# A fused gated-memory and mixture-of-experts kernel: list writes spread one by one, routing steps and weight splits at other places in the attention loop

## Chip, cores and metric

The kernel runs on one NeuronCore of one Trainium2 chip. The metric is the device time of one execution in microseconds (us), the median of the runs; less is better.

## What is computed

First a recurrent memory with exponential gates, over 4 batches, 8 heads, 768 steps and 40 columns per head. Then its 3072 output rows of 320 columns go through a two-level mixture of experts: a group (of 4) and an expert in the group (of 4) are picked by argmax, and each row is multiplied through that one expert, 320 to 1024 to 320, all in float32.

```python
for t in range(S):
    m_new = np.maximum(f_gate[:, :, t] + m, i_gate[:, :, t])
    C = f_stab * C + i_stab * np.einsum('bhd,bhe->bhde', vt, kt)
    n = f_stab * n + i_stab * kt
    y[:, :, t] = sigmoid(o_gate[:, :, t]) * (C @ qt) / np.maximum(np.abs(n @ qt), 1.0)
x = y.transpose(0, 2, 1, 3).reshape(B * S, H * D)
...
g_idx = np.argmax(x @ w_group, axis=1)
e_idx = np.argmax(xg @ w_expert[g], axis=1)
h = np.maximum(xg[mask_e] @ w1[g, e], 0.0)
out[tok_idx] = (g_w * e_w)[:, None] * (h @ w2[g, e])
```

## The kernel before

**Attention in 24 units.** A unit is one chunk of 128 steps of one batch, `u = 4 * chunk + batch`, units 0 to 23. `unit(u)` (line 795) is software-pipelined by hand, and each engine runs in the order in which the code is written. A unit loads the inputs of unit u+3 (tiles `qk`, `nt`), makes the scores of u on TensorE (`sp`), turns the finished rows of u-2 (`av<-x`, line 264), masks the scores on VectorE (`pt`, two halves, line 187), transposes the values of u-1 back (`av<-avs`), divides them on VectorE (`den`, then `xn`) and, up to unit 18, multiplies them on GpSimd into the rows `x` (line 258; from unit 19 on VectorE does that). GpSimd also scales the value rows of u+1 (`vscale`, tile `vz`, line 171), which need `nt` of that unit.

**Routing in the gaps.** After every fourth unit `logits_of` multiplies the rows by the gate matrix, and `route` (line 311) turns the logits of a set of units into a list entry per token. The sets are units 0-3, 4-7, 8-11, 12-15, 16-17, 18-21 and 22-23. `route` is a generator: each `yield` is a step of one or two small VectorE instructions (`mx`, `df`, `eq`, `oh`, rank matmul, `pr`, `slf`, `slot`, `sm`, `sg`, `se`, `ent`, `ohs`, `ohsum`). `chores` is a list of such generators, and `go_on(n)` (line 398) runs n steps of the first. The tables `FIRST`, `RANKS` and `MID` (lines 849 to 851) say how many steps each unit runs, and where in it. `first_experts` (line 457) picks the two fullest experts after the first two sets; it ends in `ewi`, the numbers that SyncE needs to load those experts' weights.

**List puts.** `put_id` (line 444) takes one unit's 128 entries and scatters them into the table `itab` in DRAM: an indirect DMA whose descriptors GpSimd writes, after a one-element memset of `sep`. Before the change every unit up to 15 puts at most one, units 16 and 17 at most two, and from unit 18 on a unit puts all that are there. When the puts of units 0 to 17 are through, SyncE reads the first expert's list back (`load_ix(0)`, tile `ix`), and GpSimd gathers its first 256 rows (`load_x`, tile `xg`). TensorE turns these rows and starts expert (0,0), while units 22 and 23 are still being routed.

**Weight splits.** Weights are split into a high and a low part in the type fp32r: `split_tasks` (line 600) lets ScalarE cast the high part (`w1h`, `wsk`, `w2h`) and puts the subtraction for the low part (`w1l`, `wsk`, `w2l`, VectorE, line 609) into the list `lows`, which `do(lows)` empties. `SPLITS` (line 852) says which units cast a part.

**After the units.** `expert((0, 0), ...)` (line 1015) runs between its matmuls four functions: `last_turn`, `last_logits`, `last_ranks` (line 981) and `last_slots` (line 996), and in the middle of its last block of the second product `late_half` (line 1007). Tokens of units 18 to 23 that belong to the first expert come in through `late_x`: VectorE makes a selection matrix per unit (`late`, line 377, a step at the end of `route`), and TensorE multiplies the rows by it (line 771). The result, split into `xhl` (lines 776, 777), is the input of expert (0,1), which has the same weights and 112 slots. Its hidden products (lines 693 to 697) go through `hs` (ACT line 698, DVE line 699) before the relu. Then experts (1,0) to (15,0) follow, each some 10 to 17 us of TensorE.

Of the kernel before, what the change touches and what calls it, by code (L numbers as in the profile page):

```python
# [61 lines left out]
def lstm_moe(ctx: ExitStack, tc: tile.TileContext, gates, qkT, nat, wcat, w1, w2, cst, seq, out):  # L62
# [59 lines left out]
    rt = {"manual": True}  # L122
# [658 lines left out]
    def run(stage, u):  # L781
        if 0 <= u < NU:
            stage(u)
# [11 lines left out]
    def unit(u):  # L795
        run(loads, u + 3)
        if u == 6:
            first_tokens()
        run(scores, u)
        run(turn, u - 2)  # L800
        go_on(FIRST.get(u, 0))
        run(lambda v: masked(v, 0), u)
        run(lambda v: masked(v, 1), u)
        if u == 0:
            busy(5)
        run(carried, u)
        run(state, u)
        run(back, u - 1)
        run(norm, u - 1)
        run(rows, u - 1)  # L810
        if u < B:
            run(rows2, u - 1)
        if u < NU - 2:
            run(vscale, u + 1)
        if u == NU - 3:
            run(vscale, u + 2)
        if u >= B:
            run(rows2, u - 1)
        if u < 12:
            sum_on(SUMS.get(u, 1))  # L820
        do(lows)
        go_on(RANKS.get(u, 0))
        if u % B == 1 and 1 < u < EUNITS:
            logits_of(u - 5, u - 1)
        if u == EUNITS + 1:
            logits_of(EUNITS - 2, EUNITS)
        if u == NU - 1:
            logits_of(EUNITS, NU - 2)
        if u == 10:
            go_on(2)  # L830
            chores.insert(0, first_experts())
        if u == EUNITS + 3:
            chores.append(early_counts())
        go_on(MID.get(u, 0))
        gate_o(u)
        do(early_splits, SPLITS.get(u, 0))
        run(state2, u)
        run(values, u)
        do(backs)
        if u == 3:  # L840
            first_entries()
        if u == 5:
            first_rows()
        for _ in range(len(ids) if u >= EUNITS else min(rt.get("old", 0), 1 if u < 16 else 2)):
            put_id()
        rt["old"] = len(ids)

    SUMS = {1: 2, 4: 2}
    FIRST = {6: 4, 10: 4, 14: 4, 18: 4, 20: 4}
    RANKS = {6: 1, 10: 1, 14: 1, 18: 1, 20: 1}  # L850
    MID = {6: 2, 7: 3, 8: 4, 10: 3, 11: 5, 12: 6, 13: 7, 14: 2, 15: 3, 16: 2, 17: 2, 18: 5, 19: 4, 20: 8, 21: 4, 22: 1}
    SPLITS = {15: 1, 16: 1, 17: 1, 20: 1, 22: 1}

    def gate_sums(lo, hi):
        fg, ig = G[:, 0, lo:hi], G[:, 1, lo:hi]
# [88 lines left out]
    with tc.manual_schedule():  # L944
        for u in range(5, NU):
            if u == NU - 1:
                rt["turns"] = turn_tasks((0, 0), EARLY, xgs[0], Cp)
            unit(u)
            if u == EUNITS + 2:
                assert not ids and len(unordered["ids"]) == EUNITS  # L950
                load_ix(0)
            do(early_loads, {12: 2, 13: 2, 15: 1, 16: 1, 17: 1, 18: 1, 20: 1, 21: 2, 22: 1, 23: 4}.get(u, 0))
            if u == NU - 3:
                xgs[0] = load_x(EARLY, ix_of(0), True)
# [24 lines left out]
            do(early_splits, 1)  # L979

        def last_ranks():
            go_on(8)
            do(early_splits)
            while ids:
                put_id()
# [10 lines left out]
        def last_slots():  # L996
            rt["experts"] = all_experts()
            next(rt["experts"])
            load_e(2, [ET.SP, ET.Pool])
            load_w1(2)  # L1000
            load_ix(2)
            load_w2(2, nc.gpsimd)
            for v in range(EUNITS, NU - 2):
                add(v)
            do(split, 1)

        def late_half():
            add(NU - 2)
            add(NU - 1)
            halves()  # L1010
            do(lows)
            do(split, 2)
            do(lows)

        expert((0, 0), EARLY, wsp_[0], xgs[0], ix_of(0), [last_turn, last_logits, last_ranks, last_slots], last=[late_half])
# [253 lines left out]
```

## Time and profile before

| | us |
|---|---|
| median of 3 runs | 379.28 (378.10 to 381.99) |
| the profiled execution, whole | 383.42 |
| its span, first to last instruction | 381.8 |
| TensorE busy in the span | 358.4 |
| VectorE, ScalarE, GpSimd busy | 248.0, 188.6, 143.0 |
| mean granted TensorE clock | 0.976 of full speed |

All rows below come from the one profiled execution, in us from the span's start. PE is TensorE's matmul, PEld its weight load, DVE VectorE, ACT ScalarE, POOL GpSimd, SP SyncE; L448 is line 448 of the kernel. In a timeline row stand start, busy time, engine, line, operation, output<-input and, in brackets, how long the engine was idle before and what ended that. "issue" is idle time for which the profile shows no cause.

### The profile page before, as it was taken

The numbers are of one execution on the slowest core, as the hardware profiler recorded it, in microseconds if no ns is written. First come the engines' busy times: TensorE is split into PE (matmuls) and PEld (weight loads), VectorE is DVE, ScalarE is ACT, GpSimd is POOL, SyncE is SP. The second block draws the span as 40 slices with busy tenths as digits, with TensorE's granted clock in tenths as the row PEclk, the third lists the DMA queues.
The fourth block names the chain that finished last, engine by engine and source line by source line (L and its number), as shares of the span: only waits on it lengthen the run. The fifth ranks groups of instructions, "written<-read, shape, count | busy, mean of one in ns | idle before, by whom it ended". The sixth has DMA issues, their size and how long they took to land.

```text
span 381.8 us, 9441 instructions
## 1 busy us (share of the span) xinstructions
PE 358.4 (94%) x3572; PEld 322.2 (84%) x3572; DVE 248.0 (65%) x639; ACT 188.6 (49%) x459; POOL 143.0 (37%) x196
## 2 busy tenths in 40 slices
PE   7999999998879779799999999999999999999993
PEld 3777777776657679799999999999999999999992
DVE  5878978887757674748895847657556633554510
ACT  2444545464334441658755737467467542454520
POOL 1263445367754045552235081332413332234110
PEclk9999999999988999889999999999999999999997
DMA  7877678889566502957079975848623497668500
GB/s 201 291 262 231 179 234 255 269 284 284 189 195 195 215 21 49 340 192 262 33 253 403 370 259 174 277 169 308 232 81 131 161 339 272 229 230 323 186 20 16
DMA packets 27383, 82.23 MB, mean 215 GB/s; under 512 B 8800, under 2 KB 12339, under 8 KB 23746
## 3 DMA queue, kind: packets, MB, share of 16 engines
q1 hardware_dynamic: 18946, 63.21, 48.8%
q0 software_dynamic: 4560, 13.16, 10.1%
q10 hardware_dynamic: 3824, 5.18, 4.1%
q8 instruction: 30, 0.49, 0.5%
q14 instruction: 23, 0.19, 0.1%
HBM read 72.70 MB, written 9.10 MB: 214 GB/s over the span
## 4 chain that ended last, share of the span: by engine, by line
PE 68%; issue 10%; DVE 7%; DMA 6%; POOL 5%; ACT 1%; POOLq 1%; SPq 0%; DVEq 0%
PE psh L714 13%; PE psh L682 8%; PE po L737 7%; PE po L738 7%; PE po L736 7%; PE sp L182 3%; PE po L742 2%; PE avT L231 2%; PE av L239 2%; PE po L741 2%; POOL x L258 2%; PE av L264 2%; PE avT L222 2%; DMA xg<-x_d,ix 2%; DMA nt<-in_nat_dram 2%
## 5 line engine op out<-in xcount | busy, mean ns | idle before, releaser
L547 POOL DMA_INDIRECT out_dram<-y,ix x32 | 38.8, 1213 | 72.8 <-ACT y L748 58.0
L736 PE MATMUL po<-w2h,hh 128*128 128x320 f32 (+3 forms) x200 | 63.4, 317 | 0.0
L737 PE MATMUL po<-w2l,hh 128*128 128x320 f32 (+3 forms) x200 | 62.3, 311 | 0.0
L738 PE MATMUL po<-w2h,hh 128*128 128x320 f32 (+3 forms) x200 | 62.1, 311 | 0.0
L543 POOL DMA_INDIRECT xg<-x_d,ix x32 | 33.7, 1052 | 74.0 <-DMA ix<-itab 40.7
L609 DVE TENSOR_TENSOR w2l<-w2s,w2h 128x640 fp32r<-128x640 f32 x64 | 50.9, 825 | 13.2 <-ACT w2h L607 13.1
L671 DVE SCALAR_TENSOR_TENSOR hh<-psh,hh 128x240 fp32r<-128x240 f32 (+6 forms) x108 | 36.2, 366 | 20.0 <-ACT hh L668 18.1
L668 ACT ACTIVATE hh<-psh 128x288 fp32r<-128x288 f32 (+8 forms) x68 | 30.1, 444 | 31.7 <-PE psh L714 15.3
L607 ACT CAST w2h<-w2s 128x640 fp32r<-128x640 f32 x64 | 43.2, 721 | 0.0
L682 PE MATMUL psh<-xhl,w1s 128*128 128x144 f32 (+3 forms) x336 | 41.3, 283 | 0.0
L682 PEld LDWEIGHTS psh<-xhl,w1s 128*128 128x128 f32 x336 | 40.9, 191 | 0.0
L714 PE MATMUL psh<-xhl,w1h 128*128 128x256 f32 (+5 forms) x224 | 37.5, 288 | 0.4 <-DVE xhl L654 0.2
L748 ACT ACTIVATE y<-po,ix 128x320 f32<-128x320 f32 (+3 forms) x24 | 12.7, 529 | 50.0 <-PE po L738 43.2
L736 PEld LDWEIGHTS po<-w2h,hh 128*128 128x128 f32 (+3 forms) x200 | 36.5, 182 | 0.0
L737 PEld LDWEIGHTS po<-w2l,hh 128*128 128x128 f32 (+3 forms) x200 | 36.4, 182 | 0.0
L738 PEld LDWEIGHTS po<-w2h,hh 128*128 128x128 f32 (+3 forms) x200 | 36.3, 182 | 0.0
L187 DVE TENSOR_TENSOR pt<-sp,cs 128x512 f32<-128x512 f32 x48 | 30.7, 680 | 5.4 <-PE sp L182 4.2
L448 POOL DMA_INDIRECT itab<-ent,slot x24 | 25.0, 1044 | 23.2 <-DVE ohs L371 17.3
L714 PEld LDWEIGHTS psh<-xhl,w1h 128*128 128x128 f32 x224 | 31.2, 189 | 1.1 <-DVE xhl L654 0.4
L258 POOL TENSOR_TENSOR x<-xn,den 128x320 f32<-128x320 f32 x19 | 18.0, 946 | 37.6 <-DVE xn L253 32.6
L182 PE MATMUL sp<-qk 40*128 40x128 f32 x384 | 29.3, 290 | 0.4 <-issue 0.4
L231 PE MATMUL avT<-pt,vz 128*41 128x128 f32 x384 | 28.1, 283 | 1.4 <-issue 1.0
(215 smaller groups left out, 706.8 us busy)
## 6 DMA issues: line engine op xcount, KB each, us to landing
w1s<-in_w_dram SPq DMA_DIRECT2D x13, 1536.0 KB
w2s<-in_w_dram SPq DMA_DIRECT2D x13, 1280.0 KB
nt<-in_nat_dram SPq DMA_DIRECT2D x24, 480.0 KB
qk<-in_qkT_dram SPq DMA_DIRECT2D x48, 160.0 KB
x_d<-x ACTq DMA_DIRECT2D x24, 192.0 KB
w1s<-in_w_dram SPq DMA_DIRECT2D x8, 384.0 KB
w2s<-in_w_dram SPq DMA_DIRECT2D x8, 320.0 KB
w1s<-in_w_dram POOLq DMA_DIRECT2D x1, 1536.0 KB
```

Of the source, the lines that this page charges most:

```text
L182: mm(t["pm"][r][:, pr, :], qk[rs, 0, pr, :], qk[rs, 1, pr, :], start=True, stop=True)
L231: mm(placed(pr, r), t["vz"][:, head(pr, r), :], t["pm"][r][:, pr, :], start=(c == 0 and pr < 2), stop=True, skip_group_check=True)
L543: return nc.gpsimd.indirect_dma_start(out=o, out_offset=None, in_=src, in_offset=bass.IndirectOffsetOnAxis(ap=idx, axis=0))
L547: return nc.gpsimd.indirect_dma_start(out=out, out_offset=bass.IndirectOffsetOnAxis(ap=idx, axis=0), in_=y, in_offset=None, bounds_check=N ...
L607: nc.scalar.copy(a, src[:, s])
L609: lows.append(lambda: nc.vector.tensor_tensor(o[rows], src[rows, s], a[rows].bitcast(F32), op=ALU.subtract))
L671: nc.vector.scalar_tensor_tensor(hh[:, f:f + per, dst], src[:, :, t], 0.0, hr.bitcast(F32)[:, :, t], op0=ALU.max, op1=ALU.subtract)
L682: ins = mm(ps[:, g * W:(g + 1) * W], w1s[:, s], xhl[:, k, :], start=(k == 0), stop=(k == 2))
L714: ins = mm(ps[:, g * W:(g + 1) * W], w[:, s], x, start=(n == 0), stop=(n == len(todo) - 1))
L736: mm(po[0:m], hh[:, f, t], w2h[:, s], start=st0, stop=False)
L737: mm(po[0:m], hh[:, f, t], w2l[:, s], start=False, stop=False)
L738: ins = mm(po[0:m], hh[:, f, tl], w2h[:, s], start=False, stop=sp0)
```

## The change

Four edits, of which none adds or removes an instruction; they move some.

- Puts: each unit ends with one `put_id`, and from unit 16 on there is another between the value rows of the next unit (`vscale`) and the rows `x`. The loop that emptied the list is gone. `load_ix(0)` comes at the end of unit 21, not 20.
- Routing: `MID` gives other numbers, and `first_experts` waits behind the route of units 4-7 instead of going ahead of it, so that the sets 4-7, 8-11 and 12-15 have their entries sooner.
- Splits in the units: `do(lows)` stands behind the `MID` steps instead of ahead of the routing, and the three parts of the first expert's `w1` are cast in units 14, 15 and 16 instead of 15, 16 and 17.
- Behind the units: `last_ranks` finishes the second generator in `chores` (the route of units 18-21, of which its four `late` tiles are left) after one step of the first (units 22-23); `last_slots` splits two parts of the next expert's `w1` instead of one, with their lows, and `late_half` the third.

```diff
         if u == NU - 3:
             run(vscale, u + 2)
+        if u >= 16:
+            put_id()
         if u >= B:
             run(rows2, u - 1)
         if u < 12:
             sum_on(SUMS.get(u, 1))
-        do(lows)
         go_on(RANKS.get(u, 0))
...
             go_on(2)
-            chores.insert(0, first_experts())
+            chores.append(first_experts())
...
         go_on(MID.get(u, 0))
+        do(lows)
         gate_o(u)
         do(early_splits, SPLITS.get(u, 0))
...
-        for _ in range(len(ids) if u >= EUNITS else min(rt.get("old", 0), 1 if u < 16 else 2)):
-            put_id()
-        rt["old"] = len(ids)
+        put_id()
...
-    SPLITS = {15: 1, 16: 1, 17: 1, 20: 1, 22: 1}
+    SPLITS = {14: 1, 15: 1, 16: 1, 20: 1, 22: 1}
...
-            if u == EUNITS + 2:
+            if u == EUNITS + 3:
                 assert not ids and len(unordered["ids"]) == EUNITS
                 load_ix(0)
...
         def last_ranks():
-            go_on(8)
+            go_on(1)
+            while next(chores[1], StopIteration) is not StopIteration:
+                pass
+            chores.pop(1)
+            go_on(7)
...
-            do(split, 1)
+            do(split, 2)
+            do(lows)
 
         def late_half():
             add(NU - 2)
             add(NU - 1)
             halves()
-            do(lows)
-            do(split, 2)
+            do(split, 1)
             do(lows)
```

On GpSimd, from unit 19 to the gather of the first expert's rows. `ent_71` are the entries of units 12-15, `ent_72` those of units 16 and 17; `vz_104`, `vz_105` and `vz_106` are the value rows of units 21, 22 and 23. Before:

```order
L447 MEMSET sep 1x1
L448 DMA itab<-ent_71,slot 49168x4
L171 TENSOR_TENSOR vz_104<-nt,eb 128x8x40
L447 MEMSET sep 1x1
L448 DMA itab<-ent_72,slot 49168x4
L447 MEMSET sep 1x1
L448 DMA itab<-ent_72,slot 49168x4
L171 TENSOR_TENSOR vz_105<-nt,eb 128x8x40
L171 TENSOR_TENSOR vz_106<-nt,eb 128x8x40
L543 DMA xg<-x_d,ix 128x384 x2
```

After the change:

```order
L171 TENSOR_TENSOR vz_104<-nt,eb 128x8x40
L447 MEMSET sep 1x1
L448 DMA itab<-ent_71,slot 49168x4
L447 MEMSET sep 1x1
L448 DMA itab<-ent_72,slot 49168x4
L171 TENSOR_TENSOR vz_105<-nt,eb 128x8x40
L171 TENSOR_TENSOR vz_106<-nt,eb 128x8x40
L447 MEMSET sep 1x1
L448 DMA itab<-ent_72,slot 49168x4
L543 DMA xg<-x_d,ix 128x384 x2
```

The last of the 18 puts now stands behind the value rows of units 22 and 23. Before, four puts of `ent_71` stood in one row ahead of `vz_104`; now one is left there, the other three having gone out between earlier rows.

On VectorE, between two low parts `hh` of expert (0,0), in `last_ranks`. `late_2475` is the selection matrix of unit 18 before, `late_2453` to `late_2459` are those of units 18 to 21 in the change; `pr` to `sm` are steps of the route of units 22-23. Before:

```order
L671 SCALAR_TENSOR_TENSOR hh<-psh,hh 128x2x256
L355 TENSOR_TENSOR pr<-av,oh 128x32
L357 TENSOR_REDUCE slf<-pr 128x2
L360 CAST slot<-slf 128x2
L363 COPY cntf<-av 128x16
L384 TENSOR_REDUCE sm<-ex 128x10
L386 TENSOR_SCALAR sm<-sm 128x10
L387 RECIPROCAL sm<-sm 128x10
L391 TENSOR_TENSOR sg<-sm,oh_2417 128x8
L393 TENSOR_REDUCE se<-sg 128x2
L395 TENSOR_TENSOR ent_74<-sm,se 128x2
L377 TENSOR_SCALAR late_2475<-cs,late_f,slf 128x112
```

After the change:

```order
L671 SCALAR_TENSOR_TENSOR hh<-psh,hh 128x2x256
L377 TENSOR_SCALAR late_2453<-cs,late_f,slf 128x112
L377 TENSOR_SCALAR late_2455<-cs,late_f,slf 128x112
L377 TENSOR_SCALAR late_2457<-cs,late_f,slf 128x112
L377 TENSOR_SCALAR late_2459<-cs,late_f,slf 128x112
L355 TENSOR_TENSOR pr<-av,oh 128x32
L357 TENSOR_REDUCE slf<-pr 128x2
L360 CAST slot<-slf 128x2
L363 COPY cntf<-av 128x16
```

Four of the six `late` instructions moved ahead of the ten routing instructions.

On VectorE, from the choice of the next experts (`ewi`) to the first hidden product of expert (0,1) (`hs`). Before:

```order
L516 CAST ewi<-eidr 128x2
L777 TENSOR_TENSOR xhl<-av,xhl 128x3x112
L609 TENSOR_TENSOR w1l<-w1s,w1h 128x1024 x2
L609 TENSOR_TENSOR wsk<-w1s,wsk 64x1024
L699 TENSOR_TENSOR hs<-hs,psh 128x112 x2
```

After the change:

```order
L516 CAST ewi<-eidr 128x2
L609 TENSOR_TENSOR w1l<-w1s,w1h 128x1024 x2
L777 TENSOR_TENSOR xhl<-av,xhl 128x3x112
L609 TENSOR_TENSOR wsk<-w1s,wsk 64x1024
L699 TENSOR_TENSOR hs<-hs,psh 128x112 x2
```

Two subtractions of the next expert's `w1` moved ahead of the input of expert (0,1).

## Rows read from the trace of the kernel before

**Rows 1.** Windows: us, busy of PE, PEld, DVE, ACT, POOL, PEclk, DMA share, GB/s

```profile
104.40:111.20 6.80, 5.08 (x62) 3.21 (x60) 3.06 (x10) 2.33 (x7) 4.44 (x9) 0.99 0.83 248
111.20:118.00 6.80, 6.53 (x55) 5.05 (x55) 6.13 (x22) 2.28 (x8) 3.73 (x5) 0.51 0.11 38
...
159.00:165.80 6.80, 5.99 (x26) 5.79 (x26) 4.76 (x13) 3.98 (x12) 0.63 (x1) 0.51 0.50 187
...
169.00:375.00 206.00, 205.76 (x1537) 201.54 (x1536) 122.22 (x257) 113.66 (x233) 62.98 (x62) 1.00 0.62 224
```

**Rows 2.** The chain that ended last, 107 to 129 us: start, us, what

```profile
107.79 0.96 POOL itab L448
...
109.52 3.60 issue
...
113.36 1.00 POOL itab L448
...
114.67 2.78 DMA itab<-ent,slot
...
117.46 1.93 DMA ix<-itab
...
121.63 6.89 DMA xg<-x_d,ix
...
128.57 0.56 PE Cp L264 x3
```

**Rows 3.** Timeline of POOL: the rows x, the put that waits, the value rows

```profile
80.80 0.72 POOL L258 TENSOR_TENSOR x<-xn,den 128x320 f32<-128x320 f32 x1 [1.41 <-DVE xn L253]
...
84.98 1.64 POOL L258 TENSOR_TENSOR x<-xn,den 128x320 f32<-128x320 f32 x1 [0.98 <-DVE xn L253]
...
113.36 1.00 POOL L448 DMA_INDIRECT itab<-ent,slot  x1 [3.83 <-DVE ohs L371]
...
115.65 1.68 POOL L171 TENSOR_TENSOR vz<-nt,eb 128x320 f32<-128x320 f32 x2
```

**Rows 4.** Timeline of DVE, 82 to 113 us

```profile
84.82 1.22 DVE L609 TENSOR_TENSOR w1l<-w1s,w1h 128x1024 fp32r<-128x1024 f32 x1
...
109.83 0.17 DVE L246 TENSOR_TENSOR den<-av,floor 128x8 f32<-128x8 f32 x1 [3.57 <-PE avT L231]
...
112.92 0.16 DVE L395 TENSOR_TENSOR ent<-sm,se 128x2 f32<-128x2 f32 x1
```

**Rows 5.** Windows of one us at the end of the loads of the units

```profile
110.00:111.00 1.00, 0.73 (x13) 0.54 (x10) 0.90 (x4) 0.58 (x2) 0.00 (x0) 1.00 0.81 270
111.00:112.00 1.00, 0.53 (x3) 0.50 (x3) 0.93 (x6) 0.25 (x1) 0.00 (x0) 0.53 0.14 45
```

**Rows 6.** Timeline of DVE, 139 to 165 us

```profile
139.63 0.69 DVE L671 SCALAR_TENSOR_TENSOR hh<-psh,hh 128x512 fp32r<-128x512 f32 x1 [0.66 <-issue]
...
142.27 1.61 DVE L377 TENSOR_SCALAR late<-cs,late_f,slf 128x112 f32<-128x112 f32 x6
...
153.74 2.35 DVE L609 TENSOR_TENSOR w1l<-w1s,w1h 128x1024 fp32r<-128x1024 f32 x2
156.12 1.22 DVE L609 TENSOR_TENSOR wsk<-w1s,wsk 64x1024 fp32r<-64x1024 f32 x1
157.37 0.45 DVE L699 TENSOR_TENSOR hs<-hs,psh 128x112 f32<-128x112 f32 x2
...
159.64 0.45 DVE L699 TENSOR_TENSOR hs<-hs,psh 128x112 f32<-128x112 f32 x2
```

**Rows 7.** Waits of PE: engine line waited for: us in total, times, longest

```profile
PE psh L693 <- DVE hs L699: 2.3, 2, 1.5
PE av L771 <- DVE late L377: 2.0, 1, 2.0
PE av L264 <- POOL sep L447: 1.9, 2, 1.2
PE Cp L264 <- DMA xg<-x_d,ix: 1.4, 2, 1.2
```

More of the change, by code (lines that the diff above doesn't have):

```diff
@@ L850, in lstm_moe @@
     RANKS = {6: 1, 10: 1, 14: 1, 18: 1, 20: 1}
-    MID = {6: 2, 7: 3, 8: 4, 10: 3, 11: 5, 12: 6, 13: 7, 14: 2, 15: 3, 16: 2, 17: 2, 18: 5, 19: 4, 20: 8, 21: 4, 22: 1}
-    SPLITS = {15: 1, 16: 1, 17: 1, 20: 1, 22: 1}
+    MID = {6: 2, 7: 3, 8: 4, 10: 2, 11: 8, 12: 8, 13: 3, 14: 2, 15: 7, 18: 7, 19: 2, 20: 8, 21: 4, 22: 1}
+    SPLITS = {14: 1, 15: 1, 16: 1, 20: 1, 22: 1}
     def gate_sums(lo, hi):
```

## The prediction

> **What bounds the kernel now.** I read the windows by stage first, then the chain that ended last, then the timelines around its longest links. From 169 to 375 us TensorE is busy for 205.76 of 206.00 us at the full clock [rows 1]: no instruction there is touched, and whatever is late before 169 us is late at the end. So the change is worth what it saves between the first unit and 169 us. In that stretch the chain does not run along TensorE's matmuls but through the list of the first expert [rows 2]: put on GpSimd, landing of the put (2.78 us), SyncE's read of the list (1.93), the gather of the rows (6.89), and only then TensorE turns the rows, at 128.57. TensorE itself got there almost at the same time; it waited 1.4 us for these rows [rows 7]. Behind them it waits 2.0 us for `late` and 2.3 us for `hs` [rows 7], and twice it runs at half clock (1.2 instead of 2.4 GHz): from 111.2 to 118.0 us, behind a stretch in which it was busy for 5.08 of 6.80 us, and from 159.0 to 165.8 [rows 1].
>
> **A. The last put.** Before, the last two puts wait for `ent` of units 16-17, done at 113.08 [rows 4], and the second goes out at 114.67 [rows 2]. `ent` is that late because VectorE sat idle for 3.57 us until 109.83 [rows 4], while GpSimd worked off four puts in a row (one of them at 107.79, rows 2) and the DMA engines were at 0.83 of their time [rows 1]. The profile gives no cause: it puts the wait down to a matmul which itself came late, and calls the 3.60 us on the chain "issue" [rows 2]. I take it for a consequence of the row of puts. With three of these four puts gone out earlier, `ent` would be ready at about 113.08 - 3.6 = 109.5, the first put runs then, and the second would go at about 110.7. But in the new order it stands behind the value rows of units 22 and 23, and these need the inputs of unit 23. The loads end at about 111.3: the DMA share falls from 0.81 to 0.14 there [rows 5]. Of the two value rows (1.68 us together, rows 3) one can run sooner, so 111.3 + 0.84 + 0.25 for the `sep` memset puts the second put at 112.4. If SyncE's loads come 1.5 us sooner, because `x` and with it the stores in the same queue lanes come sooner, it is 110.9. So A is -2.3 to -3.8 us on this execution, and 0 if the stall comes back by another cause; I take -3.0. Landing, list read and gather follow at their old lengths. A quarter of one weight load now stands ahead of the list read in SyncE's queue; the DMA engines are nearly free by then (share 0.14, rows 5), which hides it.
>
> Two more edits lie in this stretch. `first_experts` behind the route makes `ewi` about five small instructions later (1.1 us by an estimate of 0.2 us each, from `ent` and `den` in rows 4), and SyncE's weight loads with it; that delays the loads of later units, and is the reason that I don't use the upper end of A. The other is VectorE's load. GpSimd's `x` takes 0.72 us alone and 1.64 beside a `w1l` of 1.22 [rows 3, 4], and TensorE waited 1.9 us in two units for such an `x` [rows 7]. In the new order three routing steps and more stand between `xn` and the low part in unit 15, but in units 16 and 17 no step is left to stand there, so two of the three still collide; unit 18 is free of it. Against that, unit 15 carries 8 routing instructions and the 1.22 us low part behind one another, some 3 us by the same estimate, in a unit of some 4 us in which the masks and divisions take 2. I count these as +1 and -2 us on TensorE, and 0 in the sum: TensorE will be early for the rows of the first expert anyhow, and the chain of puts hides both. If that cover is gone they are worth -1.
>
> **B. The clock.** With the stall gone TensorE would not fall to half clock at 111 us, and would reach the turn of the rows about 3.6 (stall) and 3.4 us (half of 6.8) sooner than the 127.2 of before (128.57 - 1.4): at about 120, while the rows land at 128.5 - 3.0 = 125.5. That is 5 us of idle time in one piece. Idle time of 6.80 - 5.08 = 1.7 us was followed by 6.8 us at half clock before [rows 1], so expert (0,0) will begin at half clock. A full such stretch costs half of its 6.8 us, 3.4. Part of it is hidden, since in expert (0,0) TensorE waits for VectorE's routing as well; I take +1.7, bounds 0 and +3.4.
>
> The Trainium skill (TensorE: Matmul & The Clock Gate, section HAM oscillation) warns of just this: a kernel whose matmul bursts are followed by a wait for a DMA has every burst begin cold. The rows at 111.2 us agree. By that rule B is the full +3.4, which is the third rival below.
>
> **C. The `late` matrices.** Six of them took 1.61 us at 142.27, behind ten routing instructions of units 22-23, and TensorE waited 2.0 us for them [rows 6, 7]. Now four stand straight behind the `hh` that ends at 140.32 (139.63 + 0.69). They take 4 x 0.27 = 1.1 us, so at 141.4 TensorE can begin. That is when its hidden products are done: its wait of 2.0 us ended with the fourth matrix, at 142.27 + 1.1 = 143.4, so it began at 141.4. The routing behind them is 1.1 us later, its put and the next experts' choice with it; expert (0,1) hides both, since TensorE's waits name neither [rows 7]. `w2l` and the last `hh` end when they did, because VectorE's work is the same in sum, and the second product needs them in its last quarters. C is -1.9; at worst 0, if they become the wait.
>
> **D. The input of expert (0,1).** Before, VectorE did two `w1l` (2.35 us) and `wsk` (1.22) between `xhl` and the first `hs` at 157.37 [rows 6]. Now the two run beside the second product of expert (0,0), where VectorE was idle, and 1.22 is left. ScalarE's cast of `wsk` comes first, so of 2.35 us about 1.9 are won beyond C. The four pairs of hidden products follow at 159.64 - 157.37 = 2.27 us each, bound by ScalarE and VectorE as before, so the head start reaches the end of the expert. D is -1.9. It is 0 if TensorE at half clock sets the end there again, and up to -3.6 if the stretch at 159.0 does not come back (half of 3.4).
>
> **The sum.** A -3.0, B +1.7, C -1.9, D -1.9 make -5.1, from 383.42 to 378.3 for the profiled execution. The timed runs before had a median of 379.28, 4.1 below the profiled one, which is about the length of the stall; I read this as a stall that is often shorter there, and take A as -2.2 for the median: -4.3, **375.0 us**.
>
> **Rivals.**
> 1. The chain isn't shortened: the stall comes from the load on the DMA engines and not from the row of puts, or the last put waits for the inputs of unit 23 as long as it waited for `ent`. Then A and B are about 0, and half of D goes at half clock: 379.28 - 1.9 - 1.0 = 376.4, and 378 with the `ewi` delay of 1.1. For it: the profile names no cause, and the loads end at 111.3 in either case. Against it: VectorE had nothing to do for 3.57 us.
> 2. The change does what it says and the half clock at 159 us does not return: D at -3.6, B at 0. 379.28 - 2.2 - 1.9 - 3.6 = 371.6. For it, the gap for `hs` that goes; against it, pairs of 2.27 us leave TensorE half idle, as before.
> 3. Slower: TensorE waits idle for the first expert's rows and is then at half clock for the whole of expert (0,0). The place is the turn of the rows. If the inputs of unit 23 land 4 us later than before, the last put goes at 112.4 + 4 = 116.4, later than now by 1.7; expert (0,0) costs 3.4 more, and expert (0,1), again half idle, 3.4 more than the one stretch that it has. 379.28 + 1.7 + 3.4 + 3.4 - 1.9 - 1.9 = 384.0. It decides from the point where the put is later than 114.7. Against it: with `x` sooner these loads should come sooner.
>
> **How the numbers follow.** I give the forecast 0.45, rival 1 0.30, rival 2 0.13 and rival 3 0.12. Within 1% (3.8 us, about what a measurement can tell from no change) lies 375.5 to 383.1. Of the forecast's 0.45 about 0.33 lies below 375.5, of rival 1 0.02, and all of rival 2: faster 0.48. Slower is rival 3 with its 0.12, and same the rest, 0.40. The range goes from 370.5, somewhat past rival 2, to 381.0, where rival 1 with a small delay is inside and rival 3 is left out.
>
> **What would show it.** Right: no row of three or more puts between 95 and 115 us; the second put of units 16-17 at 111 to 112.5 us; TensorE idle ahead of the turn of the rows for several us, and a half clock behind it; the wait of `av` for `late` gone; the first `hs` less than 3 us behind `xhl`. Wrong: an idle VectorE of more than 2 us near 106 to 110 us with single puts (A's cause), a put of units 16-17 at 114 us or later (rival 1 or 3), a wait of `po` for `w2l` or `hh` in expert (0,0) (C), or the stretch from `xhl` to the end of expert (0,1) as long as before (D).

## The result, and the profile after

The changed kernel took **382.06 us** (median of 20 runs, 380.27 to 385.57), the kernel before 380.06 beside it (20 runs): a ratio of 1.0055, 95% interval 1.0032 to 1.0077, where 375.0 was forecast. Its profiled execution took 381.87, with a span of 380.2 (383.42 and 381.8 before). So the profile after is its kernel's median, while the profile before is 3.4 us above its own: the two traces show a gain of 1.6 us and the medians a loss of 2.0. The 383.42 is none of the 20 timed executions, and the chip it ran on is not on record. Ratios here are over executions that nothing disturbed, so they can differ a little from the ratio of two medians; for g_after below only 5 of 12 are left by that rule, because one of them is very low (376.27), and over all 12 the medians, 382.05 and 381.06, give 1.0026.

Waits of PE in the changed kernel, 60 to 170 us (in us, times, longest):

```profile
PE Cp L264 <- DMA xg<-x_d,ix: 3.9, 1, 3.9
PE av L264 <- POOL sep L447: 2.0, 1, 2.0
PE psh L693 <- DVE hs L699: 1.9, 2, 1.1
...
PE av L771 <- DVE sm L384: 0.6, 1, 0.6
```

The wait for `late` [rows 7] is gone; that for the first expert's rows has gone from 1.4 to 3.9 us; and where two waits for `sep` (in truth for `x`, ahead of it on GpSimd) were 1.2 us at most, one of 2.0 stands now. (TensorE still begins on `late` 0.55 us behind its hidden products; the name `sm` is the profile's, and the four matrices had ended at 141.49, 0.75 us before it began.) GpSimd's timeline at the new wait and at the last put:

```profile
85.13 0.72 POOL L171 TENSOR_TENSOR vz<-nt,eb 128x320 f32<-128x320 f32 x1 [2.85 <-DMA nt<-in_nat_dram]
85.79 0.09 POOL L447 MEMSET sep<- 1x1 f32 x1
86.03 1.77 POOL L448 DMA_INDIRECT itab<-ent,slot  x1 [0.16 <-issue]
87.84 0.73 POOL L258 TENSOR_TENSOR x<-xn,den 128x320 f32<-128x320 f32 x1
...
112.18 0.97 POOL L448 DMA_INDIRECT itab<-ent,slot  x1 [2.71 <-DVE ohs L371]
113.18 0.72 POOL L171 TENSOR_TENSOR vz<-nt,eb 128x320 f32<-128x320 f32 x1
114.50 0.88 POOL L171 TENSOR_TENSOR vz<-nt,eb 128x320 f32<-128x320 f32 x1 [0.59 <-DMA nt<-in_nat_dram]
...
115.56 1.00 POOL L448 DMA_INDIRECT itab<-ent,slot  x1 [0.16 <-issue]
120.32 0.97 POOL L543 DMA_INDIRECT xg<-x_d,ix  x1 [3.76 <-DMA ix<-itab]
```

At unit 16 a value row waits 2.85 us for its input; the put that the change set behind it, and ahead of `x`, takes another 1.77; only then comes `x`, whose `xn` VectorE had finished at 85.67. The last put goes at 115.56, 0.9 later than before [rows 2], and the gather at 120.32 where it went at 120.33. The windows, with the granted clock as the third figure from the end:

```profile
88.60:95.40 6.80, 6.78 (x79) 4.90 (x79) 2.12 (x5) 2.03 (x7) 4.53 (x7) 0.50 0.93 280
126.20:133.00 6.80, 5.75 (x26) 5.39 (x27) 3.72 (x13) 1.84 (x5) 0.00 (x0) 0.50 0.36 142
160.30:163.70 3.40, 3.40 (x16) 3.36 (x15) 2.50 (x6) 1.80 (x5) 0.00 (x0) 0.50 0.66 252
169.00:375.00 206.00, 203.80 (x1520) 198.95 (x1518) 121.60 (x255) 112.98 (x232) 63.43 (x63) 1.00 0.61 219
```

The half clock at 111 us [rows 1] is gone, but TensorE is at half clock (1.2 GHz) from the end of the wait at unit 16, at 88.6, and from within the wait for the rows, at 126.2; the stretch at 159 is half as long. And the loads no longer end at 111 us [rows 5], but at about 115:

```profile
111.00:112.00 1.00, 1.00 (x21) 0.74 (x20) 0.86 (x6) 0.95 (x4) 0.00 (x0) 1.00 0.88 247
...
114.00:115.00 1.00, 1.00 (x18) 0.97 (x16) 0.97 (x3) 0.54 (x2) 0.50 (x1) 1.00 0.93 349
```

VectorE in the first two experts, beside [rows 6], and TensorE's starts that answer to it:

```profile
140.42 1.07 DVE L377 TENSOR_SCALAR late<-cs,late_f,slf 128x112 f32<-128x112 f32 x4
...
147.66 2.36 DVE L609 TENSOR_TENSOR w1l<-w1s,w1h 128x1024 fp32r<-128x1024 f32 x2
...
154.47 0.27 DVE L699 TENSOR_TENSOR hs<-hs,psh 128x112 f32<-128x112 f32 x1
```

```profile
127.25 1.76 PE L264 MATMUL Cp<-cs,xg 128*128 128x128 f32 x6 [3.91 <-DMA xg<-x_d,ix]
142.24 2.90 PE L771 MATMUL av<-late,x 128*128 128x112 f32 x24 [0.55 <-DVE sm L384]
166.33 0.73 PE L714 MATMUL psh<-xhl,w1h 128*128 128x304 f32 x4
...
190.57 0.77 PE L714 MATMUL psh<-xhl,w1h 128*128 128x288 f32 x4 [0.45 <-DVE ewi L516]
```

The same four of before stand at 128.57 [rows 2], 143.28, 168.95 and, without a wait, 191.84.

### The profile page after: what moved, and what is told of

It reads as the page before. It is cut to its first block, busy times and chain, and to the rows that moved or that the text cites. A ratio compares the mean times of both kernels' runs of the same rounds, so it can differ in the third digit from the quotient of the medians.

```text
span 380.2 us, 9439 instructions
## 1 busy us (share of the span) xinstructions
PE 358.4 (94%) x3572; PEld 322.6 (85%) x3572; DVE 247.7 (65%) x639; ACT 188.5 (50%) x459; POOL 139.0 (37%) x196
## 4 chain that ended last, share of the span: by engine, by line
PE 42%; DMA 7%; issue 6%; DVE 3%; POOLq 1%; SPq 1%; POOL 1%; ACT 0%
PE psh L714 9%; PE psh L682 8%; PE po L738 5%; PE po L737 5%; PE po L736 5%; DMA ix<-itab 4%; DMA xg<-x_d,ix 3%; PE po L742 2%; PE po L741 2%; PE tp L264 1%; PE lg L264 1%; PE psh L693 1%; DVE w2l L609 1%; PE psh L696 1%; POOLq L758 1%
## 5 line engine op out<-in xcount | busy, mean ns | idle before, releaser
L547 POOL DMA_INDIRECT out_dram<-y,ix x32 | 37.4, 1169 | 71.1 <-ACT y L748 56.3
L543 POOL DMA_INDIRECT xg<-x_d,ix x32 | 33.7, 1054 | 76.6 <-DMA ix<-itab 50.8
L671 DVE SCALAR_TENSOR_TENSOR hh<-psh,hh 128x240 fp32r<-128x240 f32 (+6 forms) x108 | 36.3, 367 | 22.8 <-ACT hh L668 22.3
L714 PE MATMUL psh<-xhl,w1h 128*128 128x256 f32 (+5 forms) x224 | 38.1, 293 | 0.4 <-DVE ewi L516 0.4
L714 PEld LDWEIGHTS psh<-xhl,w1h 128*128 128x128 f32 x224 | 32.1, 194 | 0.9 <-PE psh L714 0.7
L258 POOL TENSOR_TENSOR x<-xn,den 128x320 f32<-128x320 f32 x19 | 16.2, 851 | 34.9 <-DVE xn L253 29.9
L231 PE MATMUL avT<-pt,vz 128*41 128x128 f32 x384 | 27.3, 283 | 1.3 <-DVE pt L187 1.2
L182 PE MATMUL sp<-qk 40*128 40x128 f32 x384 | 27.9, 285 | 0.0
```

The source lines that it names most:

```text
L543: return nc.gpsimd.indirect_dma_start(out=o, out_offset=None, in_=src, in_offset=bass.IndirectOffsetOnAxis(ap=idx, axis=0))
L547: return nc.gpsimd.indirect_dma_start(out=out, out_offset=bass.IndirectOffsetOnAxis(ap=idx, axis=0), in_=y, in_offset=None, bounds_check=N ...
L671: nc.vector.scalar_tensor_tensor(hh[:, f:f + per, dst], src[:, :, t], 0.0, hr.bitcast(F32)[:, :, t], op0=ALU.max, op1=ALU.subtract)
L714: ins = mm(ps[:, g * W:(g + 1) * W], w[:, s], x, start=(n == 0), stop=(n == len(todo) - 1))
```

## The experiments

Six sets, each on one chip; `before` is the kernel before on that chip. Chips have numbers.

| chip | kernel | before us | its us | ratio, 95% interval |
|---|---|---|---|---|
| 6 | e1_tail | 385.56 | 382.86 | 0.9911 (0.9872 to 0.9950) |
| 6 | e2_units | 385.56 | 384.24 | 0.9977 (0.9946 to 1.0007) |
| 6 | e3_putend | 385.56 | 381.97 | 0.9894 (0.9836 to 0.9952) |
| 6 | e4_insert | 385.56 | 380.93 | 0.9885 (0.9828 to 0.9941) |
| 1 | r_after | 387.27 | 384.01 | 0.9928 (0.9892 to 0.9964) |
| 1 | e5_both | 387.27 | 381.06 | 0.9855 (0.9807 to 0.9903) |
| 1 | e6_putfirst | 387.27 | 381.79 | 0.9873 (0.9828 to 0.9917) |
| 8 | f_after | 386.31 | 382.43 | 0.9895 (0.9850 to 0.9939) |
| 8 | f_both | 386.31 | 381.02 | 0.9863 (0.9816 to 0.9911) |
| 8 | e7_break | 386.31 | 382.14 | 0.9882 (0.9824 to 0.9939) |
| 1 | e8_breaktail | 386.82 | 382.44 | 0.9868 (0.9833 to 0.9902) |
| 15 | g_after | 381.06 | 382.05 | 0.9967 (0.9919 to 1.0015) |
| 10 | i_both | 380.66 | 381.46 | 1.0019 (0.9994 to 1.0044) |
| 10 | i_tail | 380.66 | 378.55 | 0.9936 (0.9909 to 0.9962) |

Each of these kernels has one profile. The next table has, from every profile, when GpSimd starts to gather the first expert's rows (POOL L543), when TensorE begins on `late` (L771) and on expert (1,0) (the first L714 behind expert (0,1)), and how long TensorE is at half clock in expert (0,1), all in us. r_before, g_before, f_before and h_before are profiles of the kernel before.

| kernel, chip | gather | `late` | expert (1,0) | half clock in (0,1) |
|---|---|---|---|---|
| before | 120.33 | 143.28 | 168.95 | 6.8 |
| after | 120.32 | 142.24 | 166.33 | 3.4 |
| e1_tail, 6 | 122.53 | 144.37 | 170.59 | 6.8 |
| e2_units, 6 | 122.08 | 145.90 | 172.32 | 6.8 |
| e3_putend, 6 | 120.43 | 142.09 | 168.43 | 6.8 |
| e4_insert, 6 | 119.20 | 141.11 | 163.66 | none |
| r_before, 1 | 121.59 | 145.10 | 173.08 | 6.8 |
| r_after, 1 | 118.92 | 141.19 | 167.64 | 6.8 |
| e5_both, 1 | 118.93 | 140.99 | 163.78 | none |
| e6_putfirst, 1 | 118.15 | 139.80 | 166.27 | 6.8 |
| e8_breaktail, 1 | 120.96 | 145.07 | 171.93 | 6.8 |
| g_before, 1 | 122.47 | 145.39 | 173.54 | 6.8 |
| f_before, 8 | 121.52 | 144.46 | 172.36 | 6.8 |
| f_after, 8 | 119.37 | 141.51 | 165.59 | 3.4 |
| f_both, 8 | 119.52 | 141.05 | 165.05 | 3.4 |
| e7_break, 8 | 117.55 | 140.14 | 165.84 | 6.8 |
| h_before, 15 | 117.10 | 140.81 | 167.19 | 6.8 |
| g_after, 15 | 121.75 | 143.76 | 167.85 | 3.4 |
| i_both, 10 | 120.59 | 143.15 | 167.25 | 3.4 |
| i_tail, 10 | 115.79 | 139.58 | 162.12 | none |

With the changed tail, from `late` to expert (1,0) takes 22.5 to 22.8 us where that last stretch is missing, 24.0 to 24.1 where it is 3.4 us long and 26.2 to 26.9 where it is 6.8. No row names what decides among the three.

**The two halves of the change.** e1_tail is the kernel before with only this part of the change, e2_units the change without it:

```diff
 def last_ranks():
-    go_on(8)
+    go_on(1)
+    while next(chores[1], StopIteration) is not StopIteration:
+        pass
+    chores.pop(1)
+    go_on(7)
 def last_slots():
-    do(split, 1)
+    do(split, 2)
+    do(lows)
 def late_half():
-    do(lows)
-    do(split, 2)
+    do(split, 1)
     do(lows)
```

> The units and the puts of before, and of the change only the tail: the four late matrices ahead of the last routing steps, and two w1l behind the xhl... that is, two low parts beside the second product of expert (0,0). In the changed kernel expert (1,0) began its hidden products at 166.33 us, 2.6 earlier than before (168.95), although the rows of the first expert came only 1.3 us earlier. Theory 1 (the tail gains, the units lose): with the units of before about 1.9 to 2.6 us faster than before, 377.5 to 378.2 where before has 380.06. Rival (what the tail saves is given back behind 169 us, where TensorE is busy for nearly all of the time): within 0.5 us of before, 379.6 to 380.6.

> The changed kernel with the tail of before: late matrices behind the last routing steps, two w1l between xhl and hs. Only the units part is left of the change (single puts, routing of three sets of units sooner, first_experts behind the route, low parts and splits moved). Theory 1: the units part alone loses what the tail gains and 2 us more: 382.06 + 1.9 to 2.6 = 384.0 to 384.7. Rival (the tail gives nothing): 382.06, as the whole change, within 0.5.

The tail gains 3.4 us by the ratio (0.0089 of 385.56; the interval goes from 1.9 to 4.9). The units alone lose nothing here, against the expectation, but `before` is 5.5 us slower than in the first comparison.

**Two edits of the units undone.** e3_putend has the puts of units 16 and later behind `x`; e4_insert has `first_experts` ahead of the route:

```diff
-        if u >= 16:
-            put_id()
...
-        put_id()
+        for _ in range(2 if u >= 16 else 1):
+            put_id()
```

```diff
-            chores.append(first_experts())
+            chores.insert(0, first_experts())
```

> The changed kernel with the puts of units 16 and later no longer ahead of x: two at the end of each of these units. The routing, first_experts, splits and tail stay as changed. Theory 1a (a put on GpSimd between the value rows, which wait for their input, and x makes x late): the wait of 2.05 us at 88.6 and the half clock from 88.8 to 95.6 go, so 2.0 to 5.4 us faster than the changed kernel, 376.7 to 380.0. Rival 1b (the inputs of units 17 and 18 land late, since SyncE's weight loads come late, and x waits for them in either order): 382.06 within 0.7, and the wait of vz for nt of 2.85 us stays with a wait of av for x behind it.

> The changed kernel with first_experts ahead of the rest of the route as before; everything else as changed. Rival 1b: ewi comes about 1.1 us sooner or more, SyncE's weight loads and the inputs of units 17 and 18 with it; the wait of vz of 2.85 us shrinks, and it is 2 to 4 us faster than the changed kernel, 378 to 380. Theory 1a: the put still stands between vz and x; 382.06 within 0.7, the wait of av for sep at unit 16 still there.

In both profiles the half clock at 88 us is gone and the longest wait for `sep` is 1.0 or 0.9 us, where e2_units, with the units of the change, has 2.8 on the same chip; so either edit undone takes the new wait away. In time, 0.9894 and 0.9885 aren't told from the 0.9911 of the tail alone. In e3_putend the last put goes at 112.72, 2.8 earlier than in the changed kernel, and its rows are still gathered at 120.43, for it landed late:

```profile
112.72 4.96 DMA itab<-ent,slot
117.69 1.86 DMA ix<-itab
```

A landing of 4.96 us where [rows 2] have 2.78. The weight quarter that the new order puts ahead of the list read isn't shown to be the cause: in the changed kernel, with the same quarter ahead, SyncE reads the list 2.19 us after the put goes out (115.56), and before it was 2.79 (114.67). First before, then after:

```profile
117.46 0.42 SPq L577 DMA_DIRECT2D ix<-itab  x1
```

```profile
117.75 0.40 SPq L577 DMA_DIRECT2D ix<-itab  x1
```

**The change again, both edits undone, and the last put first.** r_after is the changed kernel, r_before the kernel before for a profile. e5_both undoes both edits of above; e6_putfirst adds to it:

```diff
+        if u == NU - 3:
+            while ids:
+                put_id()
         if u < NU - 2:
             run(vscale, u + 1)
```

> The changed kernel itself once more, beside the three others on one chip. In the first comparison it was 1.0055 of before, while on the chip of the last four runs before took 385.56 and the whole change is between the parts run there (tail alone 0.991, units alone 0.998). Theory 1 (the parts add up, and the first chip is one where before loses less): 0.985 to 0.992 where before is at 385. Rival (the parts take from one another): 1.00 to 1.006 on any chip.

> The kernel before once more, for a profile beside the others on the same chip. If VectorE's stall of 3.57 us around 108 us belongs to the row of puts, it is there again, with den late by 3 to 4 us and a half clock behind it; if it came by chance in the one execution, VectorE waits less than 1 us there.

> The changed kernel with both edits undone together: first_experts ahead of the rest of the route, and the puts of units 16 and later at the end of the unit, behind x. Alone they gave 0.9885 and 0.9894 of before. Theory (two causes, that add up): inputs of unit 23 land at about 112 as in the run with first_experts ahead, no wait of av for sep above 1 us at unit 16; 3 to 4 us faster than the changed kernel. Rival (one cause with two ways to it, the late inputs): no better than either alone, within 0.7 us of them beside the changed kernel.

> The kernel with both undone, and the last put ahead of the value rows of units 22 and 23. If the last put sets when the list is read: it goes right behind the one before, at about 110.5 to 111 instead of 112.7 to 114.3, the list is read 2 us sooner and TensorE's wait for the first expert's rows (3.3 to 6.2 us in the runs with one part undone) is 2 us shorter: 1 to 2 us faster than with both undone. If the landing of the put waits for the loads that are still in the DMA engines (the put of 112.72 landed 4.96 us after its issue, that of before 2.78): the list is read no sooner than the loads end plus about 3 us, and the time is the same within 0.7.

On this chip the change is 0.7% **faster**; before took 387.27. Both edits undone give 2.8 us more (0.9928 to 0.9855), and in their profiles that gain isn't the new wait and its half clock at 90 us. Those are gone in e5_both, but the rows of the first expert are gathered at the same time in both, and TensorE begins on `late` only 0.2 us earlier. The gain comes behind that: expert (0,1) has 6.8 us at half clock in r_after and none in e5_both, and expert (1,0) begins 3.9 us earlier. First r_after, then e5_both:

```profile
118.92 0.97 POOL L543 DMA_INDIRECT xg<-x_d,ix  x1 [4.15 <-DMA ix<-itab]
141.19 2.90 PE L771 MATMUL av<-late,x 128*128 128x112 f32 x24 [0.75 <-DVE slf L357]
158.20:165.00 6.80, 6.80 (x28) 6.71 (x29) 4.48 (x11) 3.82 (x10) 1.08 (x2) 0.50 0.46 175
```

```profile
118.93 0.97 POOL L543 DMA_INDIRECT xg<-x_d,ix  x1 [4.16 <-DMA ix<-itab]
140.99 2.90 PE L771 MATMUL av<-late,x 128*128 128x112 f32 x24 [0.69 <-DVE slf L357]
157.00:164.00 7.00, 6.11 (x46) 5.75 (x45) 5.41 (x13) 4.12 (x13) 0.43 (x1) 1.00 0.60 210
```

The two edits don't add up beyond what one alone gave on chip 6. Putting the last put first moved it from 113.74 to 112.71, the gather from 118.93 to 118.15 and the start on `late` from 140.99 to 139.80, and no time with it: expert (0,1) has its 6.8 us at half clock again. That isn't the second answer of the expectation, though the time is the same: the put landed in 2.67 us, as the loads had ended by then (DMA share 0.16 from 113 us).

In r_before VectorE's stall is there: 3.68 us, with TensorE issuing one row of matmuls in pieces and the profile naming no releaser, while GpSimd issues four puts (106.35, 107.62, 108.88 among them):

```profile
107.66 0.63 PE L231 MATMUL avT<-pt,vz 128*41 128x128 f32 x7
108.68 0.27 PE L231 MATMUL avT<-pt,vz 128*41 128x128 f32 x1 [0.39 <-issue]
109.39 0.41 PE L231 MATMUL avT<-pt,vz 128*41 128x128 f32 x3 [0.44 <-issue]
110.12 0.27 PE L231 MATMUL avT<-pt,vz 128*41 128x128 f32 x1 [0.33 <-issue]
110.84 0.43 PE L231 MATMUL avT<-pt,vz 128*41 128x128 f32 x4 [0.45 <-issue]
```

**Is it the row of puts?** e7_break is the kernel before with a value row behind the second of the four:

```diff
-        for _ in range(len(ids) if u >= EUNITS else ...):
+        for _ in range(2 if u == EUNITS + 1 else len(ids) if u >= EUNITS else ...):
             put_id()
...
             run(vscale, u + 2)
+        if u == EUNITS + 2:
+            put_id()
```

> The changed kernel a third time. It was 1.0055 of before where before took 380.06, and 0.9928 where before took 387.27; in that second place before had two more stretches at half clock (88.0 to 91.4 and 146.0 to 149.5 us) than in the first profile. Theory 1: the time of before is what differs from chip to chip, since waits of 1 to 2 us decide there whether such a stretch comes, and the changed kernel is at 380 to 384 wherever it runs; so above 1.0 where before is near 380 and below 0.995 where it is above 385. Rival: the difference between the two comparisons is chance; then it lies between the two, at 0.998, whatever before takes.

> The kernel before again, for a profile on this chip. Theory 1: its stretches at half clock ahead of 170 us are two (13.6 us) where it takes near 380 to 383, four (20 us) where it takes 385 or more. The stall of VectorE at 105 to 111 us of 3.5 to 3.7 us is there in either case.

> The kernel with both edits undone (first_experts ahead, the puts of units 16 and later behind x): 0.9855 of before and 0.9927 of the changed kernel on the second chip. Theory 1: it has neither the wait at unit 16 nor the half clock at 88 us anywhere, so it is 2 to 3.5 us below the changed kernel on this chip too. Rival (its gain was the second chip's alone): within 1 us of the changed kernel.

> The kernel before with its row of four puts around 104 to 109 us broken in two: the value row of the next unit stands behind the second of them, and nothing else is changed. If the row of puts makes the stall: VectorE's wait of 3.5 to 3.7 us (105 to 111 us) is below 1.5, ent is done about 2 us sooner, the half clock at 111 us may go; 1 to 3 us faster than before. If the load on the DMA engines makes it: the wait stays at 3 us or more and the time within 1 us of before.

VectorE's `den` and GpSimd's last put on this chip, first in f_before, then in e7_break:

```profile
111.22 0.17 DVE L246 TENSOR_TENSOR den<-av,floor 128x8 f32<-128x8 f32 x1 [3.55 <-remote]
...
116.06 0.96 POOL L448 DMA_INDIRECT itab<-ent,slot  x1 [0.21 <-issue]
```

```profile
106.77 0.17 DVE L246 TENSOR_TENSOR den<-av,floor 128x8 f32<-128x8 f32 x1 [0.69 <-PE lg L352]
...
111.63 0.96 POOL L448 DMA_INDIRECT itab<-ent,slot  x1 [0.21 <-issue]
```

The stall goes, the last put goes 4.4 us earlier, and the kernel is 1.2% faster with two puts moved and nothing else (4.6 us, more than the 1 to 3 foreseen): as good as the whole change on this chip. f_both lies 1.2 us below the changed kernel, between the two answers of its expectation and hardly clear of noise. f_before has one more half-clock stretch than the profile before (145.9 to 149.4), 17 us in all ahead of 170 rather than the 20 foreseen.

**The broken row with the tail**, and one more profile of before:

> The kernel before with its row of four puts broken in two (0.9882 of before by itself) and the changed tail (0.9911 by itself); the routing, first_experts, low parts and other puts as before. If the two add up: 0.979 to 0.981 of before where before takes 385 or more, and below both kernels and below the one with first_experts and the late puts undone (0.9855, 0.9863). Rival (the two share one gain, the stretch at half clock before expert (0,1)): 0.987 to 0.989.

> The kernel before, for a profile on this chip. Where before takes 380 or so, VectorE's wait of 3.5 us around 108 us or one or two of the half-clock stretches of 3.4 to 6.8 us should be missing; where it takes 385 or more, the wait is there and the stretches ahead of 170 us make 17 us or more together.

The two don't add up: 0.9868 (0.9833 to 0.9902) overlaps the interval of either, though these were taken on other chips, and 0.981 is outside. The broken row has no stall here either, on a second chip: `den` waits 0.47 us. In e1_tail, whose row is unbroken, the stall is there (3.5 us), and it gained all the same. g_before took 387.69, with the stall (3.73 us) and 23.9 us at half clock ahead of 171.

**A chip on which before is fast.**

> The changed kernel a fourth time, on whichever chip comes. If the time of before is what varies and the changed kernel stays at 381 to 384: its ratio is above 1.0 where before takes 380 or so, and 0.985 to 0.995 where before takes 385 or more.

> The kernel before, for a profile on this chip. Where before takes 380 or so, VectorE's wait of 3.5 us around 108 us or one or two half-clock stretches are missing; where it takes 385 or more, the wait is there and the stretches ahead of 170 us make 17 us or more together.

Here it came. Chip 15 has before at 381.06 and the change at 0.9967 (0.9919 to 1.0015), no difference that can be told, so whether the ratio is above 1.0 stays open too. In h_before the same four puts in a row go out from 103.81 to 108.83, and nothing stalls: `den` waits 0.16 us, and the last put goes at 112.06. The DMA engines are at 0.98 of their time while the row goes out, where [rows 1] had 0.83 with the stall. Its lines:

```profile
106.50 0.17 DVE L246 TENSOR_TENSOR den<-av,floor 128x8 f32<-128x8 f32 x1 [0.16 <-PE av L239]
...
112.06 0.96 POOL L448 DMA_INDIRECT itab<-ent,slot  x1 [0.21 <-issue]
```

```profile
103.80:108.80 5.00, 5.00 (x80) 4.11 (x78) 4.49 (x16) 2.98 (x10) 4.32 (x7) 1.00 0.98 303
```

In the changed kernel on the same chip the last put is 3.4 us later than that, behind the value row of unit 23, and TensorE waits 7.93 us for the rows:

```profile
114.55 0.72 POOL L171 TENSOR_TENSOR vz<-nt,eb 128x320 f32<-128x320 f32 x1 [2.19 <-DMA nt<-in_nat_dram]
...
115.45 0.99 POOL L448 DMA_INDIRECT itab<-ent,slot  x1 [0.16 <-issue]
```

**The parts on such a chip.** The last set met another one, chip 10:

> The changed kernel with first_experts ahead of the rest of the route and the puts of units 16 and later behind x, a third time. Where before takes 385 or more: 0.985 to 0.988 again, at 380 to 382 us. Where before takes 380 or so, because its row of puts makes no stall there: 0.992 to 1.000, since only the tail's gain is left; above 1.000 if the units part loses there for a reason that neither edit touches.

> The kernel before with the changed tail alone, a second time (0.9911 on the chip where before takes 385.56). If the tail's gain stands by itself (late matrices earlier, two low parts out of the way of the first hs): 0.990 to 0.996 on any chip. If it is a gain only behind a stalled unit 20: within 0.3% of before where before takes 380 or so.

The tail gains by itself, 2.4 us (0.0064 of 380.66). i_both, which has the tail and the changed units with both edits undone, is 2.9 us slower than it, and at 1.0019 (0.9994 to 1.0044) no gain on before is told, nor a loss: nearest to the last clause of its expectation, a reason that neither edit touches. Its last put goes at 114.08 instead of 110.73, behind a value row that waited 3.19 us, and the rows come so much later that TensorE waits 7.33 us and is at half clock from 123.8 to 134.1, where i_tail has 125.5 to 128.9:

```profile
113.18 0.72 POOL L171 TENSOR_TENSOR vz<-nt,eb 128x320 f32<-128x320 f32 x1 [3.19 <-DMA nt<-in_nat_dram]
...
126.23 0.90 PE L264 MATMUL Cp<-cs,xg 128*128 128x128 f32 x3 [7.33 <-DMA xg<-x_d,ix]
```

```profile
110.73 0.96 POOL L448 DMA_INDIRECT itab<-ent,slot  x1 [0.21 <-issue]
...
123.10 0.55 PE L264 MATMUL Cp<-cs,xg 128*128 128x128 f32 x3 [1.71 <-DMA xg<-x_d,ix]
```

So the kernel before with the changed tail alone is faster than before on both kinds of chip, and on chip 10 it was the fastest of the three timed there, at 378.55. Beside the changed kernel it wasn't timed. The broken row with the tail wasn't run where the row makes no stall.

## Why the prediction was wrong

**The step that failed is A**, the list of the first expert 3.0 us earlier, 2.2 in the median. The start of the gather measures it. It moved from 120.33 to 120.32 in the two profiles of the first comparison, from 121.59 to 118.92 on chip 1, from 121.52 to 119.37 on chip 8, and from 117.10 to 121.75 on chip 15. So A came, at 2.7 and 2.2 us, on two chips whose before has the stall; it was nothing in the first pair, though its before has the stall, and a loss of 4.7 us where before has no stall. The gather before, and on chip 15 in h_before and g_after:

```profile
120.33 1.00 POOL L543 DMA_INDIRECT xg<-x_d,ix  x1 [2.99 <-DMA ix<-itab]
```

```profile
117.10 1.00 POOL L543 DMA_INDIRECT xg<-x_d,ix  x1 [1.78 <-DMA ix<-itab]
```

```profile
121.75 0.97 POOL L543 DMA_INDIRECT xg<-x_d,ix  x1 [5.30 <-DMA ix<-itab]
```

**Its first mistake is in the median**: "I read this as a stall that is often shorter there, and take A as -2.2 for the median". As far as the profiles go, the stall isn't shorter in some runs; it is there on some chips and not on others. In each profile of before on chips 1 and 8, and in the unbroken row on chip 6, it is 3.5 to 3.7 us, and before takes 385.6 to 387.3; there the change gains 0.7 and 1.1% (chips 1 and 8), the size of the forecast (-1.1%). In the one profile on chip 15 (h_before) and on chip 10 (i_tail, the same row) `den` waits 0.2, before takes 380.7 to 381.1, and A has nothing to take away. The first comparison's before, at 380.06, is of the second kind by its time; which of the two its runs were can't be shown, since the one profile at hand, with the stall, lies 3.4 us above that median. The sign was in hand and was read too mildly: a median 4.1 us below the profile, about the length of the very stall that A removes.

**Its second mistake is the place of the last put.** The prediction saw that it would stand behind the value rows of units 22 and 23, priced that at 112.4 us, and took "0 if the stall comes back by another cause" for A's worst. Measured: 115.56 in the first pair, and 115.45 against 112.06 on chip 15. It had put the inputs of unit 23 at 111.3, as before; they come later, and the DMA share falls only at 115 us. Why the loads end later, no run isolates. In the first pair `ent` was also only 1.2 us earlier than before instead of 3.6, for the units behind the new wait ran late: `den` of unit 18 began at 99.18, before at 95.91. The late input is rival 3's mechanism, and its point of decision (later than 114.7) was met; its price was lower, as the next points show. Along chip 15, before against after: second turn of the rows 126.26 and 129.74, start on `late` 140.81 and 143.76 (+2.95), expert (1,0) 167.19 and 167.85 (+0.66), span 379.8 and 380.3 (+0.5). The tail takes back most of what the put loses, about 1.7 of it by a half clock of 3.4 us in expert (0,1) instead of 6.8. (Rival 1's 378 is 377.5 by its own terms.)

**The cause given for the stall** was right as far as it was tried: breaking the row ends it (e7_break on chip 8, e8_breaktail on chip 1). It is half of the cause: the same row does nothing on chips 15 and 10. Rival 1's, the load on the DMA engines, doesn't make it alone: 0.98 of their time without a stall. Nor is it a late load of instructions: in the five profiles with the stall no instruction queue moves a packet from 104.6 to 115 us.

**Costs at nothing.** "A quarter of one weight load now stands ahead of the list read; the DMA engines are nearly free by then (share 0.14), which hides it": the reason was wrong, for the share is 0.88 to 0.95 until 115 us, but no cost shows in the changed kernel, where the list is read 2.19 us after the last put instead of 2.79. The late landing of e3_putend (4.96) is the only one of its kind among the last puts. The +1 to +2 us for `x` beside low parts were the right engine and the wrong collision: it was the put ahead of `x` that made TensorE wait 2.05 us, with half clock behind it from 88.6 to 95.4. The prediction had not looked at which puts stood between `vz` and `x`. That the chain of the list hides such a wait held on chip 1, where r_after (wait 1.92) and e5_both (0.86) gather at 118.92 and 118.93. In the first pair, with its longer stretch at half clock, it isn't shown.

**B** was right in place and size: TensorE idle for 3.91 us, half clock from 126.2 to 133.0. From the end of the turn of the rows to where TensorE could begin on `late` took 12.68 us (127.25 + 1.76 to 142.24 - 0.55) against 12.20 before (128.57 + 0.55 to 143.28 - 1.96); with 0.66 for the turn itself some 1.1 us, where 1.7 was taken. The rule of the Trainium skill (TensorE: Matmul & The Clock Gate, HAM oscillation), that a burst behind a DMA wait begins cold, agrees with the rows of after (3.91 us and a half clock behind it) and of i_both (7.33). The rows at 111.2, which the prediction called in for it, are another case: ahead of them the profile has "issue" [rows 2] and no DMA. The full 3.4 us that rival 3 took for it did not come; that the waits for VectorE's routing cover the rest is the prediction's reason, and no run isolates it.

**C** came: the wait for `late` fell from 1.96 to 0.55 us, 1.4 of the 1.9. **D**: from the start on `late` to expert (1,0), 25.67 us before, 24.09 after, 1.6 of the 1.9. But this is the half clock of expert (0,1), which fell from 6.8 to 3.4 us; where it stays at 6.8 with the changed tail (r_after, e1_tail, e3_putend, e6_putfirst, e8_breaktail), the same stretch takes 26.2 to 26.9 and D is nothing, as the prediction had for its lower bound. Without it, in i_tail, it is 22.54, against 26.38 in h_before on another chip: 3.8, as rival 2 had it, at its 3.6. So D's size, and most of what tells r_after from e5_both, is whether that stretch comes.

**"Whatever is late before 169 us is late at the end"** was half true. In the two profiles expert (1,0) begins 2.6 us earlier, the turn of expert (2,0)'s rows is at 175.46 against 178.06 (2.6), the next at 195.95 against 197.22 (1.3), and the span ends 1.6 earlier. What is gained meets work that isn't earlier by as much: two waits of TensorE are new, 0.43 us at 180.10 for ScalarE's `hh` and 0.45 at 190.57, which the profile puts down to `ewi` on VectorE. (That TensorE is busy for 203.80 us from 169 to 375, where it was 205.76, is no sign of it: its work ends at 373.7 instead of 375.3 there.) The part behind expert (1,0) takes 212.8 us before, 213.9 after and 215.0 in i_tail. So the tail, C and D, 3.0 us in the two traces, measures 2.4 (i_tail) and 3.4 (e1_tail).

## What to carry to other kernels

Before pricing a stall that a profile shows, hold the profiled execution against the timed runs: if it is slower by about that stall, the runs may not have it, and the forecast is a question of which kind they are. On an engine that works in order, an instruction put in a gap takes the gap's place in the queue: look at what the one ahead waits for and at what the one behind feeds, and price the wait of the one ahead, not its duration. When the transfers of a stage move later, the last of them moves too, and "the queue is nearly free by then" has to be read from the new end. And before a gain is put down to an edit, follow it along the profile to where it appears: here 3.9 us stood behind the edited stretch, in a half clock that came in one kernel and not in the other.

## What was not expected of the hardware

The same program stalls or not by the chip: four puts in a row hold up TensorE's issue, and with it ScalarE and VectorE, for 3.5 to 3.7 us in every profile with that row unbroken on chips 1, 6 and 8, and not at all in the one profile each on 15 and 10. What differs between the chips stays open; no queue or engine in the profile names it. And a put of one row of lists was followed by the list read 2.1 us (h_before) to 3.2 us (e7_break) after it went out, but by 4.97 in e3_putend, where the DMA engines were at 0.59 to 0.99 of their time from 112 to 116 us; in e6_putfirst, with the put at the same time, the loads ended at 113 and it was 2.68. Over all 24 puts of h_before, most of them issued among loads, the median landing is 5.5 us.
